# Loading batch 0's q and k by the cast queue, summing squares on ScalarE, moving batch 1's maxima later, and spreading out the second layer of chunk 0

## Chip, cores, metric

One core of a Trainium2 chip. The metric is the device time of one execution in microseconds (us), lower is better; a profile's span leaves out about 1.8 us of it. Times of "before" and of a variant are compared only from the same rounds on the same chip.

The engines: PE (TensorE, matmuls; PEld is its weight loads), DVE (VectorE), ACT (ScalarE), POOL (GpSimd, which here mainly issues the loads that cast float32 to bfloat16: the "cast queue"; v goes by the same queue without a cast), SP (SyncE, which issues plain DMAs and the DMA transposes).

## The reference, cut

```python
def _attn_ref(q, k, v, s):                    # B=8, H=8, S=576, D=64
    scores = 1/np.sqrt(D) * np.matmul(q, k.transpose(0, 1, 3, 2))
    cum = np.cumsum(np.maximum(s, 0.0), axis=-1)
    bias = -(cum[:, :, :, None] - cum[:, :, None, :])
    scores = np.where(causal, -1e9, scores + np.minimum(bias, 0.0))
    scores = scores - np.max(scores, axis=-1, keepdims=True)
    attn = np.exp(scores)
    attn = attn / (np.sum(attn, axis=-1, keepdims=True) + 1e-09)
    return np.matmul(attn, v)

x = attn_out.transpose(0, 2, 1, 3).reshape(B * S, H * D)      # 4608 x 512
h = x @ w_in                                                  # 512 -> 2048
return (0.5 * h * (1 + erf(h / sqrt(2)))) @ w_out             # 2048 -> 512
```

## The kernel before

PE works through nine chunks of 512 tokens, each with layer 1 (`l1_item`, L1 below) and layer 2 (`l2_item`, L2). Attention of batch c+1 is woven into chunk c: small pieces of it (`sc` scores and exp, `mk` causal mask, `av` attention times v, `to_xT` transpose of the result) are called from the table `side` after each sixteenth of layer 2. Batch 0's attention runs first, alone, as the start. The exponentials need no running maximum as long as q and k are small, so every q and k also goes through an absolute maximum (`absmax`) for a test at the end.

```python
def raw_qk(b):                                # two buffers, one tile per batch
    raws[b, "qk"] = work.tile([128, 2, HG, S * 2], bf16, tag="rawqk", bufs=2, name="raw_qk")

def load_qk(b, i, g0=0, n=HG):                # cast queue, float32 -> bf16
    nc.gpsimd.dma_start(out=raw_qk(b)[:, i, g0:g0+n, :], in_=qk_runs(q if i == 0 else k, b, g0, n))

def to_xT(b, it, pe=False):
    if not pe:                                # by the DMA's transpose, SP's queue
        nc.sync.dma_start_transpose(out=xT[:, :, t0:t0+n], in_=x[:n, :])
        return
    ...                                       # by PE, and a DVE copy

load_k0()                                     # k of batch 0 as float32, SP's queue
load_qk(0, 0, 0, 1); load_qk(0, 0, 1, 1)      # q of batch 0, cast queue
# ... w_in, w_out, v, batch 1's q, k
exp_set(); filler(18); cum_sum()
nc.scalar.activation(raws[0, "qk"][:, 1, 0, :], k_st[:, 0, :], func=AF.Copy)   # cast of k
weights(); filler(2)
tr_qk(0, 1, 0); tr_qk(0, 0, 0); sc_first(0, 0)
# ... the rest of batch 0's attention

for c in range(NCH):
    b = c + 1
    if c > 0 and b + 1 < B:
        load_qks(b + 1); load_v(b + 1, nc.gpsimd)
    # layer 1: per f2: l1_item(c, f2); then for c > 0:
    #   f2 < HG: tr_qk(b, 0, f2), tr_qk(b, 1, f2); f2 2, 3: scale_v(b, ...)
    #   f2 4, 5: absmax(b, f2 - 4)
    # layer 2, for c == 0:  (side[...] table in the diff below)
        groups(c, (0, 1), side[:8]); groups(c, (2,), ...); groups(c, (3,), ...)
        load_qks(2); load_v(2, nc.gpsimd)
        for g in range(HG):
            absmax(b, g)                      # batch 1
```

`filler` and `idle` are matmuls of zeros that only keep PE busy.

## Time and profile before

| | us |
|---|---|
| median of the first three runs | 325.45 (324.92 to 325.45) |
| the run that was profiled first (the one that the prediction reads) | 329.53, span 327.7 |
| all other timed executions of it, over all rounds | 322.85 to 329.51 |

The page of the profile shows PE busy in nearly every slice, so the sum to watch is when each large stage begins on PE: L1 and L2 of chunks 0, 1 and 2. Lines of a timeline are: start, duration, engine, line, operation, output<-input, count, and in brackets the idle time just before with what ended it. First the POOL timeline of the kernel before, then its DMA issues between 84 and 112 us (last column: median us from issue to landing):

```profile
72.61 0.71 POOL L106 DMA_DIRECT2D raw_qk<-in_q_dram  x1 [13.98 <-DVE rc L444]
```

```profile
raw_v<-in_v_dram POOLq DMA_DIRECT2D x8, 256.0 KB, 4.2
...
xT<-x SPq DMA_TRANSPOSE x3, 2.3
```

Batch 3's q, k are asked for at 72.61, long before PE needs batch 2's transposes, and those take 2.3 us (3.8 us in the second profile of this kernel, read below).

### The profile page before, as it was taken

How to read it: one execution, taken by the hardware profiler on the slowest of the kernel's cores; microseconds unless marked ns; L12 is line 12 of the kernel's file. 1: busy time of each engine (PE TensorE's matmuls, PEld its weight loads, DVE VectorE, ACT ScalarE, POOL GpSimd, SP SyncE). 2: the span in 40 equal slices, each digit the busy share in tenths (PEclk: the TensorE clock that was granted, in tenths of full speed). 3: DMA queues.
4: the chain of work that ended last, by engine and by line, in shares of the span. 5: the costliest groups of instructions: out<-in, count | busy, mean ns of one | idle time of the engine just before them, and what ended most of it. 6: DMA issues, size and time to landing. Idle time of an engine off the chain costs nothing. (4 is left out here: it accounts for less than half of the span.)

```text
span 327.7 us, 6109 instructions
## 1 busy us (share of the span) xinstructions
PE 311.7 (95%) x2499; PEld 160.1 (49%) x2539; DVE 205.8 (63%) x404; ACT 186.1 (57%) x248; POOL 52.0 (16%) x70
## 2 busy tenths in 40 slices
PE   7699997899999999999999999999999999999994
PEld 3247765544455445544545455545454545444441
DVE  5926688789657995796559756975697542141011
ACT  2347697228776566657495649564956495204500
POOL 8443005110605010501031103200000000000000
PEclk9659999999999999999999999999999999999999
DMA  7999923918596328531856193602210221110012
GB/s 183 259 236 207 265 35 56 293 73 152 150 200 162 108 24 187 150 117 23 199 110 152 19 211 107 159 8 82 80 34 8 82 82 32 40 67 32 1 67 72
DMA packets 30980, 37.07 MB, mean 113 GB/s; under 512 B 15648, under 2 KB 20000, under 8 KB 30944
## 3 DMA queue, kind: packets, MB, share of 16 engines
q0 software_dynamic: 11264, 22.48, 32.8%
q1 hardware_dynamic: 19536, 13.98, 14.3%
q8 instruction: 22, 0.36, 0.5%
q14 instruction: 14, 0.11, 0.2%
q10 hardware_dynamic: 144, 0.13, 0.1%
HBM read 36.85 MB, written 9.44 MB: 141 GB/s over the span
## 5 line engine op out<-in xcount | busy, mean ns | idle before, releaser
L483 PE MATMUL o_ps<-w_out_r,gT 128*128 128x512 bf16 x553 | 132.1, 380 | 2.4 <-issue 1.6
L467 PE MATMUL h_ps<-xT,w_in_r 128*128 128x512 bf16 (+1 forms) x624 | 131.5, 358 | 1.0 <-issue 0.2
L472 ACT ACTIVATE gT<-h_ps 128x1024 bf16<-128x1024 f32 (+1 forms) x80 | 74.8, 938 | 66.4 <-PE h_ps L467 65.2
L467 PEld LDWEIGHTS <-w_in_r 128*128 128x128 bf16 x640 | 59.8, 98 | 54.2 <-issue 0.6
L483 PEld LDWEIGHTS <-gT 128*128 128x128 bf16 x576 | 52.2, 98 | 57.4 <-issue 3.4
L360 ACT ACTIVATE P<-sc_ps 128x1024 bf16<-128x1024 f32 x56 | 54.3, 1021 | 30.9 <-PE sc_ps L345 30.8
L493 DVE COPY o_sb<-o_ps 128x512 f32<-128x512 f32 x32 | 22.1, 692 | 51.2 <-PE o_ps L483 51.2
L122 POOL DMA_DIRECT2D raw_v<-in_v_dram x40 | 34.0, 864 | 71.5 <-ACT sq L217 65.6
L444 DVE RECIPROCAL rc<-av 128x4 f32<-128x4 f32 (+1 forms) x80 | 14.0, 175 | 44.4 <-PE av L435 44.4
L196 DVE STREAM_TRANSPOSE qkT<-raw_qk 128x576 f32<-128x576 f32 x32 | 37.1, 1240 | 2.6 <-ACT raw_qk L515 2.6
L435 PEld LDWEIGHTS <-P 128*128 128x128 bf16 x576 | 28.3, 99 | 17.4 <-issue 1.7
L445 DVE TENSOR_TENSOR x<-av,rc 128x256 bf16<-128x256 f32 (+1 forms) x80 | 33.8, 423 | 3.0
L209 DVE TENSOR_REDUCE amx<-raw_qk 128x2 f32<-128x2304 bf16 x14 | 35.2, 2535 | 0.0
L435 PE MATMUL av<-vv,P 128*128 128x65 bf16 x576 | 31.3, 195 | 0.7 <-DVE x L445 0.4
L368 DVE TENSOR_TENSOR P<-P,tri_bf 128x1024 bf16<-128x1024 bf16 x32 | 22.0, 686 | 7.8 <-ACT P L360 7.7
L225 DVE TENSOR_TENSOR vv<-raw_v,wb 128x512 bf16<-128x512 f32 (+1 forms) x40 | 26.0, 690 | 0.0
L217 ACT ACTIVATE sq<-raw_v 128x512 bf16<-128x512 f32 (+1 forms) x40 | 24.6, 624 | 0.0
L345 PE MATMUL sc_ps<-qkT 32*128 32x256 bf16 (+2 forms) x560 | 18.8, 251 | 1.1 <-ACT P L360 1.1
L345 PEld LDWEIGHTS <-qkT 32*128 32x128 bf16 x560 | 12.2, 92 | 13.7 <-issue 12.9
L106 POOL DMA_DIRECT2D raw_qk<-in_q_dram x9 | 6.2, 693 | 73.8 <-DVE amx L209 40.2
L419 PE MATMUL f_ps<-zero 128*128 128x512 bf16 x42 | 16.4, 504 | 1.2 <-DVE zero L159 1.2
L397 ACT ACTIVATE P<-sc_ps 128x1024 bf16<-128x1024 f32 x8 | 8.2, 1023 | 10.5 <-PE sc_ps L390 10.5
(78 smaller groups left out, 102.7 us busy)
## 6 DMA issues: line engine op xcount, KB each, us to landing
out_dram<-o_sb SPq DMA_DIRECT2D x35, 256.0 KB, 2.2
raw_v<-in_v_dram POOLq DMA_DIRECT2D x32, 256.0 KB, 5.0
raw_qk<-in_q_dram POOLq DMA_DIRECT2D x7, 576.0 KB, 5.7
raw_qk<-in_k_dram POOLq DMA_DIRECT2D x7, 576.0 KB, 8.8
w_in_r<-in_moe_w_in_dram POOLq DMA_DIRECT2D x4, 512.0 KB, 11.9
w_out_r<-in_moe_w_out_dram POOLq DMA_DIRECT2D x4, 512.0 KB, 13.4
k_st<-in_k_dram SPq DMA_DIRECT2D x2, 576.0 KB, 7.4
raw_v<-in_v_dram POOLq DMA_DIRECT2D x8, 128.0 KB, 4.7
```

Of the source, the lines that this page charges most:

```text
L122: eng.dma_start(out=t[:n_st, st, :, :], in_=bass.AP(tensor=v.tensor, offset=v.offset + b * H * S * D + st * 128 * D, ap=[[D, n_st], [S * D ...
L196: nc.vector.transpose(qkT[b % 2][:, i, g, :S, :].rearrange("p s e -> p (s e)").bitcast(fp32) .rearrange("p (l j) -> p j l", j=LT), raws[b, ...
L209: nc.vector.tensor_reduce(amx[:, b * HG + g], raws[b, "qk"][:, :, g, :], axis=AX, op=ALU.max, apply_absolute_value=True,)
L217: nc.scalar.activation(sq[:n_st], raws[b, "v"][:n_st, st].rearrange("p h d -> p (h d)"), func=AF.Square, accum_out=sumv[:n_st, b, st : st ...
L225: nc.vector.tensor_tensor(vv[b % 2][:n_st, st, :, 0:D], raws[b, "v"][:n_st, st, :, :], w.unsqueeze(2).to_broadcast([n_st, H, D]), op=MULT,)
L345: nc.tensor.matmul(s_ps[h // 2][:, h % 2, off : off + n], lhsT=qk[r, 1, g, jt * 128 : jt * 128 + 128, e], rhs=qk[r, 0, g, i0 : i0 + n, e], ...
L360: nc.scalar.activation(P[:, 2 * h2 : 2 * h2 + 2, o : o + 512], s_ps[h2], func=AF.Exp, scale=scale)
L435: nc.tensor.matmul(o_ps[:, h, :], lhsT=P[:, h, off : off + 128], rhs=vv[b % 2][:, jt, 4 * g + h, :], start=(i == 0), stop=(i == len(BLK[it ...
L445: nc.vector.tensor_tensor(x_of[b, it][:n, g * 256 : g * 256 + 256].rearrange("p (h d) -> p h d", d=D), o_ps[:n, :, 0:D], rc[:n].unsqueeze( ...
L467: nc.tensor.matmul(h_ps[:, i, :], lhsT=w_in_r[:, ko, ft * 128 : (ft + 1) * 128], rhs=xT[:, ko, c * NB + n0 : c * NB + n1], start=(ko == 0) ...
L472: nc.scalar.activation(gT_of[c][:, f2 * 2 : f2 * 2 + 2, n0:n1], h_ps, func=AF.Gelu)
L483: nc.tensor.matmul(y_of[c, sub], lhsT=gT[:, ft, sub * 128 : (sub + 1) * 128], rhs=w_out_r[:, ft, :], start=(ft == 0), stop=(ft == FT - 1),)
```

## The change

Its intent: start the first scores earlier (no staged float32 k, no cast by ACT or DVE), keep PE's clock up in the start, unload DVE (batch 0's four maxima become sums of squares on ACT; batch 1's two reductions move from the end of chunk 0 into chunk 1's L2), and take the waits out of chunk 0's L2.

```diff
-    k_st = work.tile([128, FT, NB], bf16, tag="gT", bufs=1, name="k_st")   # and load_k0
-    load_k0()
-    load_qk(0, 0, 0, 1)
-    load_qk(0, 0, 1, 1)
+    for g in range(HG):
+        for i in range(2):
+            load_qk(0, i, g, 1)
...
+    ssq = const.tile([128, HG, 2], fp32, name="ssq")
+    def square_qk(g, i):
+        sq = work.tile([128, S * 2], bf16, tag="sqk", bufs=1, name="sqk")
+        nc.scalar.activation(sq, raws[0, "qk"][:, i, g, :], func=AF.Square, scale=D ** -0.5,
+                             accum_out=ssq[:, g, i : i + 1])
...   # cum negated and on ACT, the certificate's signs turned; amx of batch 0 = ssq + 0.25
-    filler(18)
+    filler(22)
     cum_sum()
-    nc.scalar.activation(raws[0, "qk"][:, 1, 0, :], k_st[:, 0, :], func=AF.Copy)
     weights()
-    filler(2)
+    filler(4)
+    filler(3, raws[0, "qk"][:, 1, 0, :128])
...   # q before k, more fillers, scores of batch 0 in another order
-                side[0] = [(sc, b, 0, 0), (absmax_half, 0, 1, 0), (mk, b, 0, 0), (scale_v, b, 0)]
-                side[2] = [(sc, b, 1, 0), (absmax_half, 0, 1, 1), (mk, b, 1, 0), (scale_v, b, 1)]
-                side[3] = [(sc, b, 0, 1), (idle, 6), (av, b, 0, 0), ... (sc, b, 1, 1), ... (idle, 4)]
...
+                side[0] = [(sc, b, 0, 0), (scale_v, b, 0), (scale_v, b, 1), (mk, b, 0, 0)]
+                side[3] = [(sc, b, 1, 0), (scale_v, b, 2), (mk, b, 1, 0)]
+                side[5] = [(sc, b, 0, 1), (av, b, 0, 0), (av, b, 0, 1), (scale_v, b, 3)]
...
+                side[7] = [(sc, b, 1, 1), (av, b, 1, 1, True), (to_xT, b, 0, True)]
...
+                side[11] = [(av, b, 1, 2, True), (scale_v, b, 4), (square_qk, 0, 0), (square_qk, 0, 1)]
+                side[12] = [(av, b, 1, 3, True), (square_qk, 1, 0), (square_qk, 1, 1)]
...
                 load_qks(2)
                 load_v(2, nc.gpsimd)
-                for g in range(HG):
-                    absmax(b, g)
...
                 if c == 1:
+                    side[0].extend([(absmax, c, 0), (absmax, c, 1)])
```

More of the change, by code (lines that the diff above doesn't have):

```diff
@@ L129, in load_v @@
             )
-    k_st = work.tile([128, FT, NB], bf16, tag="gT", bufs=1, name="k_st")
-    k_st = k_st.rearrange("p f n -> p (f n)")[:, : HG * S * 4].bitcast(fp32).rearrange("p (g c) -> p g c", g=HG)
-    def load_k0():
-        raw_qk(0)
-        for g in range(HG):
-            nc.sync.dma_start(out=k_st[:, g : g + 1], in_=qk_runs(k, 0, g, 1))
     s_sw = const.tile([64, S], fp32, name="s_sw")
     nc.sync.dma_start(out=s_sw, in_=s.flatten_outer_dims())
-    load_k0()
-    load_qk(0, 0, 0, 1)
-    load_qk(0, 0, 1, 1)
+    for g in range(HG):
+        for i in range(2):
+            load_qk(0, i, g, 1)
     w_in_r = const.tile([128, KO, dff], bf16, name="w_in_r")
@@ L200, in tr_qk @@
         )
-    def absmax_half(b, g, i):
-        nc.vector.tensor_reduce(
-            amx[:, b * HG + g, i : i + 1], raws[b, "qk"][:, i, g, :], axis=AX, op=ALU.max,
-            apply_absolute_value=True,
+    ssq = const.tile([128, HG, 2], fp32, name="ssq")
+    def square_qk(g, i):
+        sq = work.tile([128, S * 2], bf16, tag="sqk", bufs=1, name="sqk")
+        nc.scalar.activation(
+            sq, raws[0, "qk"][:, i, g, :], func=AF.Square, scale=D ** -0.5,
+            accum_out=ssq[:, g, i : i + 1],
         )
@@ L240, in cum_sum @@
         nc.vector.tensor_tensor_scan(s_pos, one, s_pos, 0.0, op0=MULT, op1=ALU.add)
-        nc.vector.tensor_scalar(cum, s_pos, s_pos[:, 287:288], None, op0=ALU.subtract)
+        nc.scalar.activation(cum, s_pos, func=AF.Identity, scale=-1.0, bias=s_pos[:, 287:288])
     def weights():
@@ L249, in weights @@
             )
-        nc.scalar.activation(wb[:, 0 : ST - 1], t_ps[:, 0 : ST - 1], func=AF.Exp)
-        nc.scalar.activation(wb[:SL, ST - 1], t_ps[:SL, ST - 1], func=AF.Exp)
+        nc.scalar.activation(wb[:, 0 : ST - 1], t_ps[:, 0 : ST - 1], func=AF.Exp, scale=-1.0)
+        nc.scalar.activation(wb[:SL, ST - 1], t_ps[:SL, ST - 1], func=AF.Exp, scale=-1.0)
     bad = const.tile([1, 1], mybir.dt.int32, name="bad")
@@ L263, in cert_exp @@
     def cert_exp():
-        nc.scalar.activation(w64, cum, func=AF.Exp)
+        nc.scalar.activation(w64, cum, func=AF.Exp, scale=-1.0)
     def cert_decay():
@@ L271, in cert_decay @@
         nc.vector.tensor_reduce(W[:, ST - 1 : ST], w64[:, 512:S], axis=AX, op=ALU.add)
-        le(goods[:, 0:1], cum[:, 0:1], -MAX_C, ALU.is_ge)
-        le(goods[:, 1:2], cum[:, 511:512], 2.0, ALU.is_ge)
-        le(goods[:, 2:3], cum[:, S - 1 : S], MAX_C)
-        le(goods[:, 3:4], cum[:, 255:256], -14.0, ALU.is_ge)
+        le(goods[:, 0:1], cum[:, 0:1], MAX_C)
+        le(goods[:, 1:2], cum[:, 511:512], -2.0)
+        le(goods[:, 2:3], cum[:, S - 1 : S], -MAX_C, ALU.is_ge)
+        le(goods[:, 3:4], cum[:, 255:256], 14.0)
         nc.vector.tensor_copy(drop[:, 0:1], W[:, 0:1])
@@ L291, in cert_1 @@
         cg[0] = g = const.tile([128, 3], fp32, name="cg")
+        nc.vector.tensor_scalar(amx[:, 0:HG, :], ssq, 0.25, None, op0=ALU.add)
         for i in range(2):
@@ L318, in cert_3 @@
         nc.vector.tensor_scalar(f, m, -2.0 * D * scale / 256, 1.0, op0=MULT, op1=ALU.add)
+        nc.vector.tensor_scalar_max(f, f, 0.0)
         for _ in range(8):
@@ L530 @@
     load_w(1, 3)
+    tr_qk(0, 0, 0)
     tr_qk(0, 1, 0)
-    tr_qk(0, 0, 0)
     sc_first(0, 0)
-    nc.vector.tensor_copy(raws[0, "qk"][:, 1, 1, :], k_st[:, 1, :])
+    filler(3)
+    masks()
+    tr_qk(0, 0, 1)
+    den_col(0)
     tr_qk(0, 1, 1)
-    tr_qk(0, 0, 1)
-    masks()
-    den_col(0)
+    sc_first(0, 1, (0,))
     filler(4)
@@ L543 @@
     scale_v(0, 1)
+    filler(2)
     sc_first(1, 0, (1,))
-    filler(1)
+    filler(2)
     av_item(0, 0, 0)
     filler(1)
+    av_item(0, 0, 1)
     mk_item(0, 1, 0)
-    sc_first(0, 1, (0,))
-    filler(1)
-    av_item(0, 0, 1)
-    filler(1)
-    sc_first(0, 1, (1,))
-    av_item(0, 1, 0)
-    filler(1)
-    sc_first(1, 1, (0,))
-    av_item(0, 1, 1)
-    filler(1)
+    sc_first(0, 1, (1,))
+    filler(2)
+    av_item(0, 1, 0)
+    av_item(0, 1, 1)
+    sc_first(1, 1, (0,))
+    to_xT(0, 0, True)
+    filler(1)
+    to_xT(0, 1, True)
     sc_first(1, 1, (1,))
-    to_xT(0, 0, True)
-    filler(2)
-    to_xT(0, 1, True)
-    filler(3)
     mk_item(0, 0, 1)
@@ L583 @@
             late = [
-                [], [], [(av, 0, 0, 2)], [(av, 0, 1, 2)], [(av, 0, 0, 3)],
+                [], [], [], [(av, 0, 0, 2), (av, 0, 1, 2)], [(av, 0, 0, 3)],
                 [(av, 0, 1, 3), (to_xT, 0, 2, True)], [(to_xT, 0, 3, True)],
                 [(scale_v, 0, 4), (av, 0, 0, 4)],
-                [(av, 0, 1, 4), (to_xT, 0, 4, True), (absmax_half, 0, 0, 0), (absmax_half, 0, 0, 1)],
+                [(av, 0, 1, 4), (to_xT, 0, 4, True)],
             ] + [[]] * 7
@@ L625 @@
                 side = [[] for _ in range(16)]
-                side[0] = [(sc, b, 0, 0), (absmax_half, 0, 1, 0), (mk, b, 0, 0), (scale_v, b, 0)]
-                side[2] = [(sc, b, 1, 0), (absmax_half, 0, 1, 1), (mk, b, 1, 0), (scale_v, b, 1)]
-                side[3] = [
-                    (sc, b, 0, 1), (idle, 6), (av, b, 0, 0), (av, b, 0, 1), (scale_v, b, 2),
-                    (av, b, 1, 0, True), (sc, b, 1, 1), (av, b, 1, 1, True), (mk, b, 0, 1),
-                    (scale_v, b, 3), (idle, 4),
-                ]
-                side[4] = [(av, b, 0, 2), (mk, b, 1, 1), (to_xT, b, 0, True)]
-                side[5] = [(av, b, 0, 3), (to_xT, b, 1, True)]
-                side[7] = [(av, b, 1, 2, True)]
-                side[8] = [(av, b, 1, 3, True), (gelu_set,), (scale_v, b, 4)]
-                side[10] = [(to_xT, b, 2, True)]
-                side[11] = [(to_xT, b, 3, True)]
+                side[0] = [(sc, b, 0, 0), (scale_v, b, 0), (scale_v, b, 1), (mk, b, 0, 0)]
+                side[3] = [(sc, b, 1, 0), (scale_v, b, 2), (mk, b, 1, 0)]
+                side[5] = [(sc, b, 0, 1), (av, b, 0, 0), (av, b, 0, 1), (scale_v, b, 3)]
+                side[6] = [(av, b, 1, 0, True), (mk, b, 0, 1)]
+                side[7] = [(sc, b, 1, 1), (av, b, 1, 1, True), (to_xT, b, 0, True)]
+                side[8] = [(av, b, 0, 2), (to_xT, b, 1, True), (gelu_set,), (mk, b, 1, 1)]
+                side[9] = [(av, b, 0, 3)]
+                side[11] = [(av, b, 1, 2, True), (scale_v, b, 4), (square_qk, 0, 0), (square_qk, 0, 1)]
+                side[12] = [(av, b, 1, 3, True), (square_qk, 1, 0), (square_qk, 1, 1)]
+                side[13] = [(to_xT, b, 2, True)]
+                side[14] = [(to_xT, b, 3, True)]
                 groups(c, (0, 1), side[:8])
@@ L643 @@
                 load_v(2, nc.gpsimd)
-                for g in range(HG):
-                    absmax(b, g)
             else:
```

## The prediction

> **What bounds the kernel now.** I read the page first. TensorE (PE) is busy 95% of 327.7 us, so from about 28 us on the kernel is bound by the order in which PE works; what can be won lies where PE works slowly or waits, and the page's slices show where.
>
> ```profile
> span 327.7 us, 6109 instructions
> ...
> PE   7699997899999999999999999999999999999994
> ...
> PEclk9659999999999999999999999999999999999999
> DMA  7999923918596328531856193602210221110012
> ```
>
> A slice is 8.2 us. The granted clock is down in slices 2 and 3 (8 to 25 us): half of the row's only gap. DMA is full until about 43 us. Next I read the stretch table, microsecond by microsecond (busy us by engine, then granted clock, DMA share, GB/s).
>
> ```profile
> 7.00:8.00 1.00, 0.69 (x5) 0.11 (x2) 0.00 (x0) 0.38 (x1) 1.00 (x2) 1.00 1.05 309
> 8.00:9.00 1.00, 0.00 (x0) 0.00 (x0) 0.18 (x1) 1.00 (x3) 1.00 (x2) 1.00 1.07 309
> ...
> 10.00:11.00 1.00, 0.00 (x0) 0.09 (x1) 1.00 (x2) 0.00 (x0) 0.36 (x1) 1.00 1.04 336
> 11.00:12.00 1.00, 0.79 (x8) 0.46 (x7) 0.97 (x3) 0.00 (x0) 1.00 (x2) 0.50 1.19 212
> ...
> 24.00:25.00 1.00, 1.00 (x10) 0.47 (x10) 0.32 (x2) 0.91 (x1) 1.00 (x2) 0.68 1.08 207
> ```
>
> PE idles from 7.7 to 11.2, and its clock is 0.50 from 11 to 24.3 us although it looks busy. The PE timeline says what it waited for and when the large stages begin:
>
> ```profile
> 7.09 0.60 PE L419 MATMUL f_ps<-zero 128*128 128x512 bf16 x2
> 11.21 1.03 PE L390 MATMUL sc_ps<-qkT 32*128 32x256 bf16 x8 [3.52 <-DVE qkT L196]
> ...
> 28.53 2.78 PE L467 MATMUL h_ps<-xT,w_in_r 128*128 128x256 bf16 x24
> ```
>
> The wait is for the transposes of k: VectorE (DVE) starts them at 8.82 after ScalarE's (ACT) cast of staged k (7.62 to 8.78), which waited for the load. Layer 1 of chunk 0 starts at 28.53; its layer 2 starts at 45.81 and chunk 1's layer 1 at 70.23 in the same timeline. Last, the DVE and POOL timelines for chunk 1, which matter below:
>
> ```profile
> 67.31 5.00 DVE L209 TENSOR_REDUCE amx<-raw_qk 128x2 f32<-128x2304 bf16 x2
> ...
> 72.95 2.32 DVE L196 STREAM_TRANSPOSE qkT<-raw_qk 128x576 f32<-128x576 f32 x2
> ...
> 81.00 5.00 DVE L209 TENSOR_REDUCE amx<-raw_qk 128x2 f32<-128x2304 bf16 x2
> 88.85 0.69 DVE L493 COPY o_sb<-o_ps 128x512 f32<-128x512 f32 x1 [2.86 <-PE o_ps L483]
> ```
>
> ```profile
> 52.98 0.70 POOL L106 DMA_DIRECT2D raw_qk<-in_q_dram  x1 [18.86 <-DVE amx L203]
> ```
>
> Batch 2's q, k may be loaded only when batch 0's last reader has left the shared buffer (52.98); before chunk 1's first output copy DVE has just 2.86 us to spare.
>
> **What the Trainium skill says.** "TensorE: Matmul & The Clock Gate", Part 1: after an idle window of about 3.4 us the clock falls to half, and it takes a busy window to return. The trace agrees with the fall (3.52 us idle, then 0.50); the return took 13.3 us here in a mix of small matmuls, while dense fillers from 1.2 us on give no sign of a half clock after 5 us. The same part's "Engine queue depths": ACT and DVE are strict FIFO; the trace shows them in program order. "DMA: Bandwidth & Descriptors", "SWDGE vs HWDGE vs iDMA": a cast in a DMA needs the GpSimd queue; hence the staged float k here needed a cast by an engine. The same page, "Queues, rings and completion order": an engine takes turns between queues. The trace agrees: raw_qk (cast queue) and k_st (SP) of group 0 land together, at 7.42 and 7.60 in the landing records.
>
> **The change part by part.**
>
> (1) q, k of batch 0 by the cast queue. The packet records give 0.19 us for a packet of either queue, 8 packets per engine and load, so a load is 1.5 us of all engines. Sequential instead of side by side, q group 0 should land near 5.9, but k group 0 after the same bytes as now: about 7.5. The gain is the removed casts: ACT 1.16 and DVE 0.95 (L534), and that q is transposed before k lands. Transpose of k: 7.6 to 8.85 (1.24 each). PE's queue ahead: 22 instead of 18 fillers (4 x 0.22 more, end 7.6), 0.5 of cum transposes, 4 fillers, 3 on the landed k: to 9.5. First scores at about 9.5, not 11.21.
>
> (2) The clock. No gap of 3 us is left in PE before 9.5, so I expect full clock from the warm-up on. I followed the chain with full-clock durations from the rows after 25 us: a half scores item 0.45 to 0.63, exp 1.02, mask 0.69, scale_v 0.65, av 0.25 to 0.41, normalising 0.6, xT copy 0.42. Exps end at 11.0, 12.0, 13.1, 14.3, 15.4, 17.5, 19.4 and 20.9 (the middle ones wait for the two score banks, k of group 1 landing at 10.5, v landing at 11.9, and the mask ahead of av); xT of the first 256 tokens is done at 19.9. Layer 1 starts at about 20.1: 8.4 us earlier. Its weights do not hold it: w_in lands at 14.3, 16.9, 20.8, 23.7 and PE wants the parts at 20, 22, 24 and 26.
>
> (3) Layer 1 of chunk 0 stays 17.2 us (PE bound, 17.28 now): layer 2 from 37.4.
>
> (4) Layer 2 of chunk 0, spread. Now 24.42 us. Work: 64 matmuls x 0.216 = 13.8; scores 2 x 0.6 + 2 x 0.75 = 2.7; eight av, 2.3; four xT transposes, 1.0; that is 19.8. The rest now is 1.1 of idle fillers (removed) and waits for exps. In the new order, each scores item comes at least 1.7 us of layer 2 after the one before; I find only about 1 to 1.5 us of waits: about 21.2 us, gain 3.2. w_out parts 2 and 3 land at 41.7 and 44.2 and are wanted at about 42.2 and 45.4: just hidden. Chunk 1's layer 1 starts at 58.6 instead of 70.23: **gain 11.6 us**.
>
> (5) What is given back. ACT takes four squares of 128x1152 (1.12 by the slope between the 512 and 1024 wide ACT rows, plus 0.1 to 0.2 for reading the sum: 4 x 1.25 = 5.0), in FIFO behind the copy of sub-tile 2's output, which ends 16.8 us into layer 2: they end at 59.2. The buffer of batch 2's q, k is released only then, 6.2 us later than the 52.98 of now although everything else is 11.6 earlier. From issue to landing it was 5.75 (q) and 9.25 (k, counted from q's issue): k lands at 68.4. DVE in order: transpose of k 1.2, normalising 0.6, two transposes 2.3, five scale_v 3.2 (to 75.7), then four absmax reductions, as batch 1's two have moved behind: 10.0, to 85.7; output copy 0.6, mask 0.6: 86.9. PE's av of batch 2 (91.91 now, 80.3 shifted) needs that mask: **a wait of 6.6 us**. It is over 3.4 us, so the clock should fall again and return after one or two windows of 3.4 us: 1.7 to 3.4 us more, weighted 2.2.
>
> (6) Cum on ACT, negated constants, one more scale and max in the certificate: below 0.3 us or off the path.
>
> Sum on the unprofiled time: 325.45 - 8.4 - 3.2 + 6.6 + 2.2 = 322.6; I choose 322.0, as DVE's order might leave a bit more room than I found.
>
> **Rivals.** A: no give-back, because batch 2's loads come earlier than I think or PE finds other work. Then 325.4 - 11.6 = 314. For it: the change was meant to unload DVE, and the first 60 us do get shorter. Against: buffer and queue order leave no other reading, and the order of DVE's instructions puts all four reductions ahead of the copy. B: the clock falls in the start anyway, since scores use 32 rows of the array and small fillers may not count; in the trace a mix like this, called busy, did not raise the clock for 13 us. Layer 1 would start near 26: 325.4 - 2.5 - 3.2 + 6.6 + 2.2 = 328.5. Against: the mix at 50 to 60 us, busy 80%, kept the clock at 1.00. C: DMA becomes the bound, with w_out 1 us later than thought and a wait of 1 to 2 us in layer 2: 324. D: the give-back without the clock's fall: 320.
>
> **Range and chances.** Main path 0.65 with a spread of 3 us around 322; A 0.15; B 0.1; C and D the rest. Range 315.5 to 327. Faster by over 2% means below 318.9: A, and the fast tail of the main path: 0.27. Slower means over 332: 0.03.
>
> **What would show each step.** Right: granted clock 1.00 from 5 to 75 us; first scores near 9.5, layer 1 near 20, layer 2 near 37.4, chunk 1 near 58.6; the POOL issue of batch 2's q near 59, waiting for ACT's squares; DVE idle for raw_qk until about 68; PE waiting some 6 us for the mask of batch 2 near 80 to 87, with a half clock after it. Wrong: no such PE wait (A), a clock of 0.50 between 10 and 20 us (B), PE waiting for w_out_r (C).

## The result, and the profile after

337.85 us median of four runs (335.3 to 341.48), against 325.45 before: 3.4% slower (ratio 1.0338, 95% interval 1.0239 to 1.0437). A ratio here is the mean time of one kernel's fast runs over the mean of the other's fast runs of the same rounds, later profiled runs left out, so not quite the ratio of the medians. The profiled run of these, 341.48 us, counts as slow (over 1.5% above the fastest of its kernel). The same code was therefore run again at the end (`g2_after_again`, all four runs fast, 340.14 us, ratio 1.0434 in its own rounds). The lines below are from that profile; the first one shows the same waits (10.40 and 6.63 us instead of 9.74 and 6.75).

From the page of the changed kernel (40 slices of 8.5 us):

```profile
span 338.5 us, 6150 instructions
...
PE   8999999996292999999999999999999999999993
...
PEclk9999999999589699999999999999999999999999
```

The start is now dense and at full clock. All damage is in slices 10 to 14, about 76 to 118 us. The PE timeline has both holes:

```profile
10.56 0.62 PE L388 MATMUL sc_ps<-qkT 32*128 32x256 bf16 x8
...
22.23 3.66 PE L465 MATMUL h_ps<-xT,w_in_r 128*128 128x256 bf16 x32
...
39.52 1.03 PE L481 MATMUL o_ps<-w_out_r,gT 128*128 128x512 bf16 x4
...
59.42 1.89 PE L465 MATMUL h_ps<-xT,w_in_r 128*128 128x512 bf16 x8
...
91.00 0.40 PE L433 MATMUL av<-vv,P 128*128 128x65 bf16 x4 [9.74 <-DVE P L366]
...
110.25 3.57 PE L465 MATMUL h_ps<-xT,w_in_r 128*128 128x512 bf16 x8 [6.75 <-issue]
```

The hole before 91.00 is the mask wait that the prediction had. The one before 110.25 it did not have. The eight matmuls after it take 3.57 us where the same eight took 1.89 at 59.42: the clock is at half. The table of stretches of the same run shows that (stretch, length, busy us of PE, PEld, DVE, ACT and POOL, clock, DMA share, GB/s):

```profile
90.00:92.00 2.00, 1.00 (x6) 0.50 (x7) 1.47 (x4) 0.00 (x0) 2.00 (x4) 0.50 1.12 209
...
106.00:108.00 2.00, 0.00 (x0) 0.00 (x0) 0.00 (x0) 0.00 (x0) 0.69 (x1) 1.00 1.31 73
...
112.00:114.00 2.00, 2.00 (x12) 0.90 (x11) 0.00 (x0) 0.14 (x1) 0.00 (x0) 0.50 1.03 281
```

From 106 to 108 us no engine computes (POOL's 0.69 is the end of its issuing of v) and the DMA engines are fully busy; so a transfer is the likely end of the second hole, which e8 below tests. (Its line says "issue": the profile found no releaser. In two experiments below the same hole is put down to the DMA of xT.) Next the DVE, POOL and DMA views of the same run that correspond to those of before:

```profile
72.84 1.26 DVE L187 STREAM_TRANSPOSE qkT<-raw_qk 128x576 f32<-128x576 f32 x1 [1.74 <-DMA raw_qk<-in_k_dram]
...
79.83 9.91 DVE L204 TENSOR_REDUCE amx<-raw_qk 128x2 f32<-128x2304 bf16 x4
89.67 0.67 DVE L491 COPY o_sb<-o_ps 128x512 f32<-128x512 f32 x1
90.27 0.67 DVE L366 TENSOR_TENSOR P<-P,tri_bf 128x1024 bf16<-128x1024 bf16 x1
```

```profile
61.13 0.70 POOL L106 DMA_DIRECT2D raw_qk<-in_q_dram  x1 [26.71 <-ACT sqk L198]
...
85.12 0.71 POOL L106 DMA_DIRECT2D raw_qk<-in_q_dram  x1 [18.35 <-DVE amx L204]
...
90.71 0.77 POOL L106 DMA_DIRECT2D raw_qk<-in_q_dram  x1
```

```profile
raw_v<-in_v_dram POOLq DMA_DIRECT2D x8, 256.0 KB, 9.7
...
xT<-x SPq DMA_TRANSPOSE x2, 10.5
```

Batch 3's q, k are now asked for at 85.12 instead of 72.61, after a wait for DVE's reductions, and batch 4's follow at 90.71. So loads of batches 3 and 4 stand in one row just when SP issues the transposes of batch 2 (98.08). These take 10.5 us instead of 2.3 or 3.8.

Where a profile of *before* was needed for the sum, I used one taken again (`f4_before_again`, span 322.0), because the first turned out not to be typical. Its PE timeline:

```profile
11.09 0.63 PE L390 MATMUL sc_ps<-qkT 32*128 32x256 bf16 x8 [2.15 <-DVE qkT L196]
...
23.05 2.78 PE L467 MATMUL h_ps<-xT,w_in_r 128*128 128x256 bf16 x24
...
64.75 1.89 PE L467 MATMUL h_ps<-xT,w_in_r 128*128 128x512 bf16 x7
...
97.13 1.89 PE L467 MATMUL h_ps<-xT,w_in_r 128*128 128x512 bf16 x8
```

Here PE waits 2.15 us instead of 3.52 before the first scores, the clock stays at 1.00, and layer 1 begins at 23.05 instead of 28.53. The two executions are of one and the same kernel; the first one happened to lose its clock (more on this under "What stays open").

Starts of the stages on PE in us, from the PE timelines ("-": not used here):

| run | L1 c0 | L2 c0 | L1 c1 | L2 c1 | L1 c2 | L2 c2 | span |
|---|---|---|---|---|---|---|---|
| before, first profile | 28.53 | 45.81 | 70.23 | 84.52 | 102.61 | 117.39 | 327.7 |
| before, again | 23.05 | 40.33 | 64.75 | 79.05 | 97.13 | 111.91 | 322.0 |
| after (fast profile) | 22.23 | 39.52 | 59.42 | 73.72 | 110.25 | 127.54 | 338.5 |
| e1 (squares undone) | 22.31 | - | 59.83 | 74.13 | 106.38 | - | 335.1 |
| e2 (batch 1's maxima back) | - | 40.04 | 60.5 | 74.8 | 100.6 | 115.4 | 325.6 |
| e3 (both) | 21.71 | 39.00 | 60.58 | 74.88 | 92.96 | 107.75 | 318.4 |
| f2 (both, tile padded) | 21.84 | 39.12 | 59.02 | 73.32 | 91.40 | 106.18 | 316.9 |

After against before again: start −0.8, L2 of chunk 0 −4.5 (19.90 against 24.42), chunk 1's L2 +18.5 (36.53 against 18.08), chunk 2's L1 +2.5 (17.29 against 14.78), the rest +0.8; in sum +16.5, the difference of the spans. That is more than the medians differ by (337.85 - 325.45 = 12.4; 340.14 - 325.73 = 14.4 in the rounds of g2), since the profile of before is of one of its faster executions (323.81). The question is thus what fills 18.5 us in one stage.

### The profile page after: what moved, and what is told of

It is laid out like the page before. It is cut to its first block, busy times and chain, and to the rows that moved or that the text cites. A ratio compares the mean times of both kernels' runs of the same rounds, so it can differ in the third digit from the quotient of the medians.

```text
span 339.7 us, 6150 instructions
## 1 busy us (share of the span) xinstructions
PE 314.1 (92%) x2538; PEld 158.7 (47%) x2538; DVE 200.7 (59%) x400; ACT 190.2 (56%) x256; POOL 52.8 (16%) x72
## 5 line engine op out<-in xcount | busy, mean ns | idle before, releaser
L465 PE MATMUL h_ps<-xT,w_in_r 128*128 128x512 bf16 (+1 forms) x640 | 135.2, 363 | 6.6 <-issue 6.6
L481 PE MATMUL o_ps<-w_out_r,gT 128*128 128x512 bf16 x576 | 137.5, 383 | 1.2 <-DMA w_out_r<-in_moe_w_out_dram 1.2
L465 PEld LDWEIGHTS <-w_in_r 128*128 128x128 bf16 x640 | 60.5, 99 | 62.3 <-issue 10.1
L187 DVE STREAM_TRANSPOSE qkT<-raw_qk 128x576 f32<-128x576 f32 x32 | 37.6, 1243 | 10.5 <-DMA raw_qk<-in_q_dram 8.5
L433 PEld LDWEIGHTS <-P 128*128 128x128 bf16 x576 | 27.6, 99 | 28.1 <-DVE P L366 11.5
L212 ACT ACTIVATE sq<-raw_v 128x512 bf16<-128x512 f32 (+1 forms) x40 | 24.6, 624 | 0.0
L417 PE MATMUL f_ps<-zero 128*128 128x512 bf16 x49 | 14.3, 423 | 1.2 <-DVE zero L150 1.2
## 6 DMA issues: line engine op xcount, KB each, us to landing
raw_v<-in_v_dram POOLq DMA_DIRECT2D x8, 128.0 KB, 10.5
```

Source lines behind the costliest of these rows:

```text
L187: nc.vector.transpose(qkT[b % 2][:, i, g, :S, :].rearrange("p s e -> p (s e)").bitcast(fp32) .rearrange("p (l j) -> p j l", j=LT), raws[b, ...
L212: nc.scalar.activation(sq[:n_st], raws[b, "v"][:n_st, st].rearrange("p h d -> p (h d)"), func=AF.Square, accum_out=sumv[:n_st, b, st : st ...
L433: nc.tensor.matmul(o_ps[:, h, :], lhsT=P[:, h, off : off + 128], rhs=vv[b % 2][:, jt, 4 * g + h, :], start=(i == 0), stop=(i == len(BLK[it ...
L465: nc.tensor.matmul(h_ps[:, i, :], lhsT=w_in_r[:, ko, ft * 128 : (ft + 1) * 128], rhs=xT[:, ko, c * NB + n0 : c * NB + n1], start=(ko == 0) ...
L481: nc.tensor.matmul(y_of[c, sub], lhsT=gT[:, ft, sub * 128 : (sub + 1) * 128], rhs=w_out_r[:, ft, :], start=(ft == 0), stop=(ft == FT - 1),)
```

## The experiments

All outputs are right. The theory at the outset was the prediction's own: ACT's squares release batch 0's buffer late, DVE falls behind, PE waits for the mask. The rival was that the moved reductions of *batch 1* do it, by way of the buffers; later two more came up, that the buffers' addresses cost transfer time, and that the start's gain was never there to be had. Expectations are quoted as they were written before each run.

### Undoing the two suspects: e1, e2, e3, e4

`e1_dve_absmax0`: batch 0's sums back to DVE maxima, as before; everything else of the change stays.

```diff
-                side[11] = [..., (square_qk, 0, 0), (square_qk, 0, 1)]
-                side[12] = [..., (square_qk, 1, 0), (square_qk, 1, 1)]
+   # absmax_half of batch 0 in late[8], side[0] and side[3]
```

> The changed kernel with one part undone: batch 0's absmax stays on VectorE at its old places, so no squares; batch 1's absmax stays in chunk 1's layer 2. Theory (late release): batch 2's q, k load is issued before 50 us instead of 61.4, lands before chunk 1 starts, and PE's wait for the mask of batch 2 falls from 10.4 us to 2 us or less; batch 3's load still takes batch 2's buffer and still bunches, so a wait for xT at the start of chunk 2 may remain, up to 6 us. About 317 to 324 us. Rival (cast queue or new order slow in themselves): above 330 us, with the wait still there.

336.46 us (before in the same rounds 324.88; ratio 1.0296): an expectation missed by far. The mask wait is gone, and the *other* one has grown. PE, POOL and DMA (76 to 110 us) of this run:

```profile
106.38 3.57 PE L470 MATMUL h_ps<-xT,w_in_r 128*128 128x512 bf16 x8 [13.84 <-issue]
```

```profile
46.16 0.70 POOL L106 DMA_DIRECT2D raw_qk<-in_q_dram  x1 [11.14 <-DVE amx L204]
...
75.90 0.71 POOL L106 DMA_DIRECT2D raw_qk<-in_q_dram  x1 [24.09 <-DVE amx L210]
```

```profile
xT<-x SPq DMA_TRANSPOSE x2, 15.8
```

Batch 2's load is issued at 46.16, so the squares did hold it until 61.13. But batch 3's still waits, for DVE's reductions, and the transposes of batch 2 take 15.8 us. The squares alone do not explain the result.

`e2_absmax1_back`: only batch 1's two reductions go back to the end of chunk 0; the squares stay.

```diff
                 load_v(2, nc.gpsimd)
+                for g in range(HG):
+                    absmax(b, g)
...
-                    side[0].extend([(absmax, c, 0), (absmax, c, 1)])
```

> The changed kernel with the other part undone: batch 1's absmax back at the end of chunk 0's layer 2; the squares stay where the change has them. Theory: VectorE does these 5 us while it waits for batch 2's q, k, so PE's wait for the mask falls by 5 us, from 10.4 to 5 or 6; batch 3's load takes batch 1's buffer and comes near 67 us instead of 86, so the transposes by DMA land in 2 to 4 us and the wait of 6.6 us at chunk 2's start goes. About 321 to 326 us. Rival (only the late squares matter): about 334 us, second wait unchanged.

326.19 (before 324.88; ratio 0.9986, interval 0.9896 to 1.0076): level with before. The second wait is gone and the first is down to

```profile
87.89 0.40 PE L433 MATMUL av<-vv,P 128*128 128x65 bf16 x4 [5.54 <-DVE P L366]
```

because two reductions fewer stand ahead of the mask. One move of the change, not examined in the prediction's step 5 for what it does to the *loads*, carries most of the loss.

The mechanism is in the built program. A tile with two buffers takes the place of an earlier one, and which it takes is settled when the program is built. The offsets of the q, k tiles in the two programs:

```
          batch 2   batch 3
before    152064    161280
after     135712    135712
```

Before, batch 3 takes the other buffer than batch 2. In the changed kernel batch 1's last reader (the moved reductions, in chunk 1's layer 2) stands in the program after the place where batch 3's tile is allocated (at the top of chunk 1), and batch 3 gets *batch 2's* buffer. (The built programs of e1 and g1, too, give both batches one offset, 135712 and 152064; those of e2 and e3 give them two.) Its load must then wait until batch 2 has landed, been transposed and been reduced: it goes 25.7 us after chunk 1's start (85.12 − 59.42) instead of 2.4 (72.61 − 70.23).

`e3_both`: e1 and e2 together.

> Both undone: no squares, batch 1's absmax at its old place, the rest of the change kept. Theory: no long wait in chunk 1 or 2, clock 1.00 from 5 us on, all of the start's gain of 10.5 us is kept: 314 to 316 us. Rival (half of the loss is elsewhere): 320 us or more.

319.43 (before 324.88; ratio 0.9778, interval 0.9692 to 0.9865). No mask wait, no xT wait. Slower than expected: I had still counted the start as a large gain. Each undoing alone leaves a loss (+11.6 and +1.3 us by the medians), together they win 5.5: two waits in a row on one path, of which the longer one hides part of the other.

`e4_old_layer2`: e3 with the old table of chunk 0's layer 2.

```diff
-   # the spread side[0], side[3], side[5] ... side[14]
+   # before's side[0], side[2], side[3] ... side[11]
```

> As e3_both, but chunk 0's layer 2 in the old order. Separates the start from the spread: layer 1 of chunk 0 begins at 21.5 as in the changed kernel, layer 2 takes 24.4 us again instead of 20.9. Theory: 3 to 3.5 us slower than e3_both, 318 us. Rival (the spread gains nothing): equal to e3_both.

322.9: the difference to e3 is as expected, so the spread table is worth 3.5 us in the time (322.9 − 319.43, same rounds); the 318 itself was missed, as e3's time was.

### The transposes and the clock: e8, e6

`e8_pe_transposes`: the changed kernel, but batch 2's first two transposes of x on PE instead of by DMA.

```diff
+                    side[9][-1] = (av, b, 1, 0, True)      # no DMA transpose after it
+                    # likewise (av, b, 1, 1, True) in side[10]
+                    side[11].append((to_xT, b, 0, True))
+                    side[12].append((to_xT, b, 1, True))
```

> The changed kernel, with batch 2's first two x tiles transposed by PE instead of by DMA, nothing else. Theory (second wait is the DMA transposes queued among the bunched loads): the wait of 6.6 us at chunk 2's start and the half clock after it go, the wait of 10.4 us for the mask stays; 8 to 10 us less than the changed kernel, about 328 us. Rival (chunk 2 waits for something else, or is late as a result of the first wait): no change.

332.09 (before 325.41; ratio 1.0222), some 4 us above what I expected. With no DMA transpose there, chunk 2's layer 1 follows without a wait:

```profile
105.42 1.89 PE L465 MATMUL h_ps<-xT,w_in_r 128*128 128x512 bf16 x8
```

So the second hole was indeed these transfers. The mask wait stays, at 10.17 us.

`e6_warm`: e8 with 90 matmuls of zeros on PE ahead of the mask wait.

```diff
+                    side[5].append((idle, 90))
```

> As e8_pe_transposes, plus 90 small matmuls on zeros where PE waits for the mask (9.9 us at 0.11 us, inside the wait of 10.4). They change no data; they keep PE active. Theory (the half clock after the wait costs): clock stays 1.00 and it is 2 to 3 us faster than e8_pe_transposes. Rival (half clock costs nothing here): same or slower.

329.77, 2.3 us less than e8 (332.09, same rounds), as expected. The clock rows of the two pages, e8 and then e6:

```profile
PEclk9999999999769999999999999999999999999998
```

```profile
PEclk9999999999999999999999999999999999999999
```

The zeros fill the wait for the mask (10 us of them from 80.28) and the clock never falls. The half clock after one such wait costs about 2.3 us by the medians (the two kernels' runs overlap in one, 332.48); the prediction had 2.2.

### Squares earlier, and the start: e9, e10

`e9_early_squares`: e2 with the squares moved up to the middle of the layer, so that the buffer is free sooner.

```diff
+                side[2] = [(square_qk, 0, 0)]
+   # (square_qk, 0, 1) at the end of side[3]; (square_qk, 1, 0), (square_qk, 1, 1) at the end of side[8]
```

> The changed kernel with the squares kept on ScalarE but earlier (one after each of the first two scores, two after the last exps of chunk 0's layer 2) and batch 1's absmax at its old place. Theory (it is the place of the squares, not their cost, that hurt): batch 2's load is issued near 55 us, no long wait, 314 to 317 us. Rival (squares as such cost): 2 us or more slower than e3_both.

321.93 (before 325.41; ratio 0.9916). The mask wait is down to 0.40 us, so for this wait it matters *where* the squares stand, not that they are on ACT. It missed its expectation: a wait of 1.88 us for xT remained at chunk 2's layer 1, and the start's gain was again counted too high. Against before it gains 3.5 us and e3 5.5, a difference of 2.0 us, which is what the rival named. In the trace it goes with the xT wait: batch 4's load is issued at 81.07 (79.06 in e3), and the transposes take 6.3 us (2.8). That the squares on ACT cost nothing is not shown.

`e10_before_bridged`: the kernel before, with more zeros ahead of the first scores.

```diff
-    filler(2)
+    filler(18)
```

> The kernel before with one edit: 18 instead of 2 fillers after the cum transposes, which fill PE's gap from 7.7 to 11.2 us; loads and casts as before. Theory (most of the start's gain is the clock): clock stays 1.00 from 5 us on, layer 1 of chunk 0 starts at 22 to 23.5 instead of 28.5, 319 to 321 us. Rival (the gain is the removed casts and loads): 324 to 325 us.

324.11 (before 325.41; ratio 0.998, interval 0.9914 to 1.0047). Missed: I expected the whole 5 us between a start at 28.53 and one at 23. The variant's layer 1 does start at 23.04, and its profiled run (323.92) is no slower than its timed ones, so profiling costs nothing. What was wrong is the base: an ordinary timed run of before *already* starts at about 23 to 24. The half clock at the start befalls some executions (329.53 in the first profile) and not others (323.81). The mean granted clock of each run: of the 28 timed runs of before in the four sets of rounds, 8 lie at 0.979 to 0.983 as the first profile does (0.979), one at 0.988, 13 at 0.993 to 0.995 (f3's profile, at 0.994, starts layer 1 at 23.90), and 6 at 0.998 or more as the second does (0.998). So the prediction's start was that of about one execution in four.

### The buffers' addresses: f1, f2, f3, f4

`ssq` is a new tile of 16 bytes per row. It takes 32 and moves everything allocated after it: `raw_v` lay at offset 172800, a multiple of 256, and now lies at 156448, 32 past one. (The rest of the move, 16384 bytes down, is the tile `gT`, which the staged k had made come first.) The packet records show v's 4096-byte packets at 262 to 302 ns (median of each run with the shift) instead of 194. The q, k buffers and x, which the DMA transposes read, are shifted by the same 32 bytes, but their packets did not change: 192 ns for 2304 bytes of q or k, 18 ns for 256 bytes of a transpose, in every run. v is moved in runs of 256 bytes (64 floats of one head) and q, k in longer ones, which may be why v alone pays; no run separates that.

`f1_aligned`: the changed kernel with that tile padded to 256 bytes.

```diff
-    ssq = const.tile([128, HG, 2], fp32, name="ssq")
+    ssq = const.tile([128, 64], fp32, name="ssq")[:, : 2 * HG].rearrange("p (g c) -> p g c", g=HG)
```

> The changed kernel with its new 16-byte tile of sums of squares made 256 bytes long, nothing else; this moves the v and q, k buffers behind it from 32 bytes past a multiple of 256 bytes back to a multiple. In all kernels with that tile the v packets of 4096 bytes took 265 to 307 ns (median), in the kernel before and in e10_before_bridged 195. Theory (the shift slows loads): v packets back at 195 ns, batch 2's k lands 9.3 instead of 11.7 us after q's issue, PE's wait for the mask shrinks by 2 to 3 us and the bunched loads are over sooner, so the second wait shrinks or goes; 5 to 9 us faster than the changed kernel, 328 to 332 us. Rival (the packets are slow for another reason, such as the order of loads): packets at 300 ns, 336 us.

333.26 (before 324.73; ratio 1.0259, just outside what I expected). v's packets are back at 194 ns. The PE timeline:

```profile
90.25 0.40 PE L433 MATMUL av<-vv,P 128*128 128x65 bf16 x4 [9.26 <-DVE P L366]
...
105.77 1.89 PE L465 MATMUL h_ps<-xT,w_in_r 128*128 128x512 bf16 x8 [3.17 <-DMA xT<-x]
```

The xT wait is halved, and this time the clock stays up: the eight matmuls take 1.89 us. How much that is in the time depends on which rounds of the changed kernel it is held against: its ratio to before is 1.0259 instead of 1.0338 or 1.0434, that is 2.6 or 5.7 us of 325. The first is not clear of noise (the intervals, 1.0204 to 1.0313 and 1.0239 to 1.0437, overlap).

`f2_both_aligned`: e3 with the same padding.

> e3_both (no squares, batch 1's absmax at its old place) with the same padding. Theory: w_out lands 2 to 3 us sooner, its wait of 1.2 to 1.7 us in chunk 0's layer 2 goes: 1 to 2 us faster than e3_both, 317.5 to 318.5 us, the fastest so far. Rival: equal to e3_both, 319.4 us.

319.01 (before 324.73; ratio 0.9834, interval 0.9801 to 0.9867), half a microsecond above the range expected. It beats both kernels, before by 1.7%. Against e3 the profiled span is 1.5 us shorter (318.4 to 316.9), and a wait of 1.89 us for w_out in chunk 0's layer 2 is gone; the medians, from different rounds, differ by 0.4 us only, so what the padding is worth here in the time is not shown. In its DMA view the transposes of x take 2.4 us.

`f3_before_shifted`: the kernel before, with a dummy 16-byte tile.

```diff
+    pad = const.tile([128, 4], fp32, name="pad")
+    nc.vector.memset(pad, 0.0)
```

> The kernel before with a 16-byte tile more, which shifts its v and q, k buffers to 32 bytes past a multiple of 256. Theory: v packets go from 195 to about 300 ns, in a kernel with the old order of loads; the time grows little, 0 to 2 us, because the loads are hidden there. Rival: packets stay at 195 ns.

Six runs, three counted slow (clock 0.975); the fast ones 325.2, 323.44 and 327.71. The fast ones' mean is within 0.3% of before's. v's packets take 302 ns here too, so the address is the cause of that. Its time is mixed up with starts at half clock: from layer 1 of chunk 0 on, the profiled run takes 299.5 us (323.4 − 23.90) against 299.0 in f4. So before has room for slow v packets; the changed kernel, where v's packets run beside the transposes, has less (f1).

`f4_before_again`: the kernel before, unchanged.

> The kernel before once more, to see its start in another execution: the first profile was taken on a run of 329.5 us, while the timed runs lie at 323 to 328. Theory (the stretch at half clock differs between executions[...]): another length or place of the half clock, and a layer 1 start of chunk 0 between 23 and 28.5 us. Rival: the same 13.7 us at half clock, layer 1 at 28.5, so that the profile itself costs the 4 us.

325.17 (ratio 1.0046, interval 0.999 to 1.0103): a check on the method, and the profile used above.

### The one line alone, and the changed kernel again: g1, g2

`g1_before_absmax1_late`: the kernel before, with only batch 1's reductions moved as in the change.

```diff
-                for g in range(HG):
-                    absmax(b, g)
...
+                    side[0].extend([(absmax, c, 0), (absmax, c, 1)])
```

> The kernel before with one part of the change: batch 1's absmax moved from the end of chunk 0's layer 2 into chunk 1's layer 2. In the built program batch 3's q, k tile then has batch 2's address instead of batch 1's. Theory (buffer): batch 3's load is issued near 80 us, after batch 2's reductions, not at 72.6; its loads, v and batch 4's loads run in a row to about 104 us, the DMA transposes of batch 2 near 97 us land after 5 us or more instead of 2.5, and PE waits 1 to 8 us at the start of chunk 2; 327 to 334 us, slower than before by 1% or more. Rival (the second wait of the changed kernel needs the late squares or the earlier start): within 1 us of before.

333.51 median; fast runs 330.92 and 330.72, two more slow (336.11, 337.14), so no ratio. Before in the same rounds: 325.73. The PE and POOL timelines:

```profile
102.42 3.34 PE L467 MATMUL h_ps<-xT,w_in_r 128*128 128x512 bf16 x8 [4.98 <-DMA xT<-x]
```

```profile
80.80 0.71 POOL L106 DMA_DIRECT2D raw_qk<-in_q_dram  x1 [27.66 <-DVE amx L209]
```

In a kernel with neither squares, nor a new start, nor shifted buffers, that one move makes batch 3's load wait until 80.80 (72.61 before), the transposes take 8.8 us, PE wait 4.98 us, and the clock fall (3.34 us for eight matmuls). It costs 5 us in the fast runs; in the other two the granted clock is lower (0.974 and 0.969 against 0.992), so there it cost more.

`g2_after_again`: the changed kernel, unchanged.

> The changed kernel once more. Theory: in a fast execution the same two waits, for the mask 9 to 10.5 us and for xT 2 to 6 us, with a half clock after at least the first; 335 to 338 us and 12 to 17 us slower than f2_both_aligned, of which the mask and xT waits make at least 11.

340.14; its profile is the one read above. It is 2 us above the upper end of what I expected, and 2.3 above the first rounds' median. It is 21 us above f2 (other rounds), where 12 to 17 were expected; its two waits come to 16.5 us, where at least 11 were expected.

## Why the prediction was wrong, point by point

| step | predicted, us | measured, us | from |
|---|---|---|---|
| 1, 2 start | −8.4 | −0.8 | L1 c0, 22.23 against 23.05 |
| 4 layer 2 spread | −3.2 | −4.5 | L2 c0, after against before again |
| 5 wait for the mask | +6.6 | +9.7 | PE timeline |
| 5 half clock after it | +2.2 | +2.0 | what is left of chunk 1's L2, 18.5 − 9.7 − 6.8 (e8 − e6: 2.3) |
| not in it: wait for xT | 0 | +6.8 | PE timeline |
| not in it: half clock after that | 0 | +2.5 | L1 c2, 17.29 against 14.78 |

The measured rows add up to +15.7; with +0.8 after chunk 2's L1 they are the 16.5 us between the two spans. The predicted rows add up to −2.8. Of the 19.3 us between, 9.3 are the second wait and its half clock, 7.6 the start, and 3.1 the size of the mask wait. So two steps failed: (5) left out a wait, and (1, 2) counted a gain that most executions do not have.

**Start (1, 2): right in what happens, wrong in what it is worth.** First scores at 10.56 (predicted 9.5; 9.84 in the changed kernel's first profile), clock 1.00, layer 1 at 22.23 or 21.51 (predicted 20.1): the step's picture holds within about 2 us. But its 8.4 us were counted from a start at 28.53, which is an unlucky execution's, and then subtracted from 325.45, the median of executions that mostly do not have it. e10 shows the difference: a bridged start at 23.04 is only 1.3 us better by the medians, and within its interval level with before. The numbers to see it were there: the profiled run took 329.53 us, and the time to be predicted was 325.45. The 4 us between them belonged to that one execution, and I subtracted them from runs that mostly did not have them. (A small misreading beside it: a clock of 0.68 in the stretch from 24 to 25 us puts the return at 24.6, not 24.3; nothing hangs on it.)

**Layer 1 of chunk 0 (3): right.** 17.29 us against the 17.2 expected.

**Spread layer 2 (4): right, a little small.** 4.5 us by the profiles, 3.5 us by e4 against e3.

**Mask wait (5): right mechanism, mis-sized terms.** The buffer of batch 2 is released by ACT's squares (61.13, predicted 59.2), k lands 11.7 us after q's issue (9.25 counted), and the four reductions then run from 79.83 to 89.7, ahead of the output copy and the mask, as the order of DVE's instructions said. The mask is thus ready 4.0 us later than counted (90.9 against 86.9), PE asks for it 1.0 us later (81.3 against 80.3), and the wait is 9.7 us instead of 6.6. The longer landing is mostly not the address: with v's packets back to normal in f1 it is still 11.2 us. Its cause is open: an output store shares the engines at that time, which no run separated.

**The step that failed most is in (5): "what is given back" stopped at the mask.** It says that batch 1's two reductions "have moved behind", and counts only DVE's time for them. It does not ask which buffer those late reads keep and who gets another one for it. The result is batch 3's q, k in batch 2's buffer, a load 25.7 us into chunk 1 instead of 2.4, transposes of x behind it, 6.8 us of waiting and a second half clock of 2.5 us, where the prediction had 0. Shown by e1 (squares gone, wait of 13.84 remains), e2 (line moved back, wait gone), e8 (no DMA transpose, wait gone) and g1 (line alone, wait there).

**Not in it at all: a 16-byte tile changed the speed of v's transfers.** f1 puts this at 2.6 to 5.7 us of the total in the changed kernel; most of its effect is on the xT wait (6.75 to 3.17 us, and no half clock). In a kernel with room for it (f3) it costs about 0.5 us after the start, by one profile of each.

**Small items (6)** were right as far as seen: nothing of the cum's negation shows up on the path.

**The rivals.** A (no give-back) fell with the mask wait; f2, at 319.01, is the nearest to it and still 5 us above the 314 I gave it, again by the start. B (half clock in the start) fell. C (w_out late) happened in some executions only: PE waits 1.20 us for w_out in the changed kernel's first profile and 1.89 us in e3, not in g2's. D (give-back with no half clock) fell: the clock did fall, and e6 shows what that is worth. None of the four, nor the range, allowed for a second wait: the chance of 0.03 for slower was far too sure for a change with many parts and shared buffers.

**What the best version is.** f2: new start and spread layer 2, batch 1's reductions and batch 0's maxima where they were, the tile padded: 319.01 against 324.73, 1.7% (f2's own interval 1.3 to 2.0%).

**What stays open.** k's landing (above); why g2 is slower than the first rounds of the same code by 2.3 us; and what decides which executions start at half clock. On the last, four profiles of this start fall in one order (before, f3, g1, f4). The first 18 fillers take 5.51, 6.19, 6.61 and 6.76 us; PE then waits 3.52, 2.55, 2.27 and 2.15 us for the first scores; and the clock is at half for 13.7, 3.4, 0 and 0 us. The sooner the clock comes up, the sooner the fillers are done, and the longer is the gap before scores that wait for k in any case (they begin at 10.92 to 11.21). The Trainium skill ("TensorE: Matmul & The Clock Gate", Part 1, "What's actually happening") says that the window of about 3.4 us runs freely, so that the same kernel meets it at another phase each time. The runs agree with that, but none tests it. On the addresses, the Trainium skill ("DMA: Bandwidth & Descriptors", "How a descriptor splits into AXI transactions") says a descriptor that does not start at a multiple of 256 bytes is split further, and this for reads; the runs show a cost on the writing side in SBUF, 194 to 302 ns a packet in f3, which agrees in direction, but for v's packets only.

## What to carry to other kernels

When a read of a shared buffer is moved later, work out which later tile takes which buffer, at what time its load may go, and what that load will then run beside; the built program's addresses answer the first in a minute. A small new constant tile can shift the load buffers behind it: look at their packets' times before and after, and pad the tile if they grew (here v's did, those of q and k did not). And before a gain is subtracted from a median, check that the profile that it was read in is of a run near that median: a start at half clock that only some executions have is not there to be won.

## What the Trainium skill lacked or had wrong

- "DMA: Bandwidth & Descriptors" gives no cost for a load into SBUF rows that lie 32 bytes off a multiple of 256: v's packets of 4096 bytes took 262 to 302 ns instead of 194 (f1 and f3 against the changed kernel and before), those of the cast loads of q and k, shifted alike, stayed at 192 ns. Its account of the split at 256 bytes speaks of reads. "SBUF — State Buffer", "Operand start alignment", says that its runs timed nothing.
- "TensorE: Matmul & The Clock Gate", "What's actually happening", puts the ramp's penalty below 1% of a typical span. A clock that is lost again after the ramp can cost more: in the first profile of before layer 1 began 5.5 us later than in the second (28.53 against 23.05), 1.7% of 329.5. The half clock after one 10 us wait is 2.3 us, 0.7% (e8 − e6).
- The same section has the clock come back after at least one busy window of about 3.4 us; it does not say how busy a window must be. After the mask wait full clock came at 94.9 us, 3.9 us after PE resumed, in the changed kernel, and at 92.6, 4.7 us after, in e2. In the start of before's first profile it took some 13.5 us (11.2 to 24.7) of small matmuls that the profile calls busy, in f3 with the same matmuls 3.4 us (12.4 to 15.8). Every half-clock stretch inside a run lasted 3.4, 6.8, 10.2, 13.7 or 17.1 us, so a whole number of 3.41.
- No page has a figure for a DMA transpose beside loads on another queue: 2.3 us from issue to landing in before (3.8 in its second profile), 8.8 in g1, 10.5 in the changed kernel, 15.8 in e1. The turn-taking between queues that "DMA: Bandwidth & Descriptors" tells comes with no time.
